# A smaller first token group in a fused attention and feed-forward kernel: batch 0's first 256 queries go first

## The chip, the cores and the metric

The kernel runs on one core of one Trainium2 chip. The metric is device time in microseconds (us), from the first to the last instruction, so lower is better. A few words for the engines: PE is the tensor engine, ACT is ScalarE, DVE is VectorE, POOL is GpSimd, and SP is SyncE, which here only starts transfers.

## The reference

Two stages, with the output of the first as the input of the second.

```python
# q, k, v: (8 batches, 12 heads, 448 tokens, 64), float32
scores = (1 / sqrt(64)) * q @ k.transpose(0, 1, 3, 2)
attn   = maximum(scores, 0) ** 2 / 448
x      = (attn @ v).transpose(0, 2, 1, 3).reshape(3584, 768)
# w_in: (768, 2048), w_out: (2048, 768)
h   = x @ w_in
out = (h * sigmoid(1.702 * h)) @ w_out      # (3584, 768), float32
```

There is no softmax: every score is clipped at zero and squared by itself.

## The kernel before

**Units of work.** Four heads of one batch are a *quad*; there are 3 quads for each batch, 24 in all. A quad's q and k are transposed, then come seven *score slots*, one for each block of 64 keys: PE makes scores, ACT clips them (`rl`, relu), DVE squares them (`at`), and after the seventh slot PE multiplies by v (`av`) and DVE copies the result into `xt`, the input of the feed-forward stage. That stage works on *token groups* of several 64-token blocks. For each group there are 16 chunks of the first product (`ht`, 6 matmuls each; ACT applies the GELU, POOL scales into `gt`), and for each 128 tokens two output chunks (`op`, 16 matmuls each; DVE scales into `osb`, which is stored). PE's order is written out by hand. A *visit* puts up to three attention items between the feed-forward chunks.

The list of groups, in blocks of 64 tokens, and the buffers that the argument needs (3 PSUM buffers for scores and values, 2 for products and transposes):

```python
gblk = [6, 8] * (B // 2)
...
ps_s = ctx.enter_context(tc.tile_pool(name="ps_s", bufs=3, space=bass.MemoryType.PSUM))
ps_m = ctx.enter_context(tc.tile_pool(name="ps_m", bufs=2, space=bass.MemoryType.PSUM))
```

Quads 0 to 5 are loaded by POOL and transposed by PE. From quad 6 on the loads, the transposes and the stores are all started by SP:

```python
def load_qk(u):                       # quads 6 and on
    ...
        nc.sync.dma_start(out=x, in_=quad(t, b, pr))
def trans(u):
    ...
        nc.sync.dma_start_transpose(out=t[:, :, :], in_=...)
def store(g, m, lo, hi, engs): ...    # m2() passes (nc.sync, nc.sync)
def sp_gate(src):                     # SP waits here until src is there
    nc.sync.dma_start(out=gate[0:1, :], in_=src)
```

The opening. All 21 slots of batch 0 come first, then group 0's first product with quads 3 to 5 in between, then the gate with the first loads for SP, and then group 0's first output chunks:

```python
while pos[0] < b0:
    visit(1)                          # quads 0 to 2, transposes of 1, 2, 3 after slots 4, 11, 19
    ...
for f in range(NF):
    m1(0, f)
    if f in (2, 8):
        trans_pe(4 + f // 8, "k", 0)
        trans_pe(4 + f // 8, "q", 0)
    ...
    if f % 2 == 1 or f > 12:
        visit(min(3, b1 - pos[0]))
while pos[0] < b1:
    visit(min(3, b1 - pos[0]))
...
sp_gate(wout[0][1][0:1, 0, 0:64])
prefetch(8, 0)                        # q, k, v of quads 6 and 7 (SP, POOL)
for m in range(gblk[0] // 2):
    m2(0, m, 0)                       # the h = 1 halves are mixed into group 1
```

## Time and profile before

| | before |
|---|---|
| time, median of the first 3 runs | 409.68 us (408.52 to 409.70) |
| PE busy | 383.3 of 406.5 us (94%) |
| last `xt` copy releases group 0's first product | 32.15 us |
| group 0's first product and quads 3 to 5 done | 64.04 us |
| first slot of quad 6 | 77.81 us |
| group 1's first product and group 0's outputs done | 113.95 us |
| from there to the end | 292.6 us, PE nearly always full (busy for 287.7 us) |

How to read it: after 114 us only PE's own work counts. What the change can win lies in the first 114 us, where the trace has PE busy for 95.6 us and idle for 18.3. The lines themselves stand in the prediction below.

### The profile page before, as it was taken

The page shows a single profiled execution, that of the slowest core. Times are in us where ns is not written, and L with a number is a line of the kernel's source. Part 1 is how long each engine was busy: PE and PEld are TensorE (multiplying, and loading weights), DVE is VectorE, ACT ScalarE, POOL GpSimd, SP SyncE. Part 2 cuts the span into 40 slices and gives each one's busy share as a digit, 9 for nine tenths or more (in the row PEclk, how much of TensorE's full clock was granted, in tenths as well). Part 3 has the DMA queues.
Part 4 walks back from the last instruction along what each step waited for, and adds up shares of the span by engine and source line. Part 5 has one row for each costly group of instructions (what it writes and reads, how often), then busy time and mean ns, then how long its engine had stood idle before and what let it go on. Part 6 is the DMA issues. An engine that isn't in the chain of part 4 may idle for free.

```text
span 406.5 us, 7792 instructions
## 1 busy us (share of the span) xinstructions
PE 383.3 (94%) x3192; PEld 202.2 (50%) x3192; DVE 190.7 (47%) x294; ACT 205.3 (51%) x297; POOL 130.8 (32%) x200
## 2 busy tenths in 40 slices
PE   3777899899999999999999999999999999999995
PEld 2433455344455455444455555444455555455564
DVE  0894763267746565564466455546354321010121
ACT  4984771576866454556475446546745511322100
POOL 8453424434433143244133324312311222323100
PEclk9989999999999999999999999999999999999999
DMA  8999997589775653955747396845121111111133
GB/s 122 194 204 205 205 290 153 115 192 246 184 173 111 165 139 72 261 106 134 183 70 166 71 198 153 197 51 82 40 52 35 39 40 40 40 39 40 39 79 78
DMA packets 65220, 50.85 MB, mean 125 GB/s; under 512 B 35744, under 2 KB 61728, under 8 KB 65184
## 3 DMA queue, kind: packets, MB, share of 16 engines
q1 hardware_dynamic: 47792, 35.60, 35.5%
q0 software_dynamic: 17152, 14.55, 24.0%
q8 instruction: 25, 0.41, 0.4%
q10 hardware_dynamic: 240, 0.20, 0.2%
q14 instruction: 11, 0.09, 0.1%
HBM read 45.61 MB, written 11.01 MB: 139 GB/s over the span
## 4 chain that ended last, share of the span: by engine, by line
PE 84%; DVE 6%; ACT 5%; issue 2%; DMA 2%; POOL 0%; ACTq 0%; DVEq 0%; POOLq 0%
PE op L278 35%; PE ht L249 33%; PE sc L144 7%; PE av L169 7%; ACT rl L158 4%; DVE at L159 3%; DMA q<-in_q_dram 1%; DVE rl L155 1%; DVE xt L186 1%; DMA qT<-q 1%; ACT gf L254 1%; DVE kT L134 1%; DVE k L101 0%; POOL gt L256 0%; PE tr L127 0%
## 5 line engine op out<-in xcount | busy, mean ns | idle before, releaser
L158 ACT ACTIVATE rl<-sc 128x896 f16<-128x896 f32 x165 | 144.8, 920 | 49.7 <-PE sc L144 49.7
L249 PE MATMUL ht<-xt,win 128*128 128x384 f16 (+1 forms) x768 | 158.4, 353 | 4.4 <-DVE kT L134 3.4
L159 DVE TENSOR_TENSOR at<-rl 128x896 f16<-128x896 f16 x168 | 114.9, 692 | 87.7 <-ACT rl L158 87.4
L256 POOL TENSOR_SCALAR gt<-gf 128x384 f16<-128x384 f32 (+1 forms) x128 | 77.6, 606 | 235.7 <-ACT gf L254 234.7
L278 PE MATMUL op<-wout,gt 128*128 128x384 f16 (+1 forms) x912 | 153.2, 323 | 0.0
L254 ACT ACTIVATE gf<-ht 128x384 f32<-128x384 f32 (+1 forms) x128 | 70.4, 550 | 119.6 <-PE ht L249 106.8
L278 PEld LDWEIGHTS <-gt 128*128 128x128 f16 x912 | 88.0, 98 | 60.5 <-issue 2.7
L249 PEld LDWEIGHTS <-win 128*128 128x128 f16 x768 | 71.1, 98 | 81.6 <-issue 21.4
L284 DVE TENSOR_SCALAR osb<-op 128x384 f32<-128x384 f32 (+1 forms) x57 | 31.3, 549 | 108.0 <-PE op L278 106.5
L144 PE MATMUL sc<-qT,kT 64*64 64x448 f16 x672 | 48.6, 367 | 6.8 <-DVE qT L134 3.0
L169 PE MATMUL av<-at,v 64*64 64x448 f16 x672 | 38.0, 360 | 2.3 <-ACT rl L158 1.4
L144 PEld LDWEIGHTS <-kT 64*64 64x64 f16 x672 | 17.5, 107 | 33.2 <-issue 22.9
L186 DVE CAST xt<-av 128x768 f16<-128x768 f32 (+2 forms) x36 | 26.9, 774 | 8.4 <-PE av L169 8.3
L169 PEld LDWEIGHTS <-v 64*64 64x64 f16 x672 | 20.1, 109 | 16.9 <-issue 7.1
L88 POOL DMA_DIRECT2D v<-in_v_dram x24 | 17.9, 745 | 5.2 <-DMA win<-in_moe_w_in_dram 2.9
L101 POOL CAST q<-qst 128x896 f16<-128x896 f32 x18 | 16.9, 941 | 0.3
L101 DVE CAST k<-kst 128x896 f16<-128x896 f32 x18 | 14.0, 785 | 0.0
L127 PE MATMUL tr<-ident,k 128*64 128x128 f16 x84 | 4.2, 253 | 5.2 <-DMA k<-in_k_dram 5.2
L134 DVE COPY qT<-tr 128x896 f16<-128x896 f16 (+1 forms) x6 | 3.4, 572 | 7.0 <-ACT qT L132 7.0
L127 PEld LDWEIGHTS <-k 128*64 128x64 f16 x84 | 3.1, 128 | 6.9 <-DMA k<-in_k_dram 5.2
L296 POOL DMA_DIRECT2D win<-in_moe_w_in_dram x8 | 5.4, 674 | 2.3 <-DMA q<-in_q_dram 1.3
L116 POOL DMA_DIRECT2D q<-in_q_dram x6 | 4.3, 713 | 3.0 <-PE sc L144 1.3
(17 smaller groups left out, 26.2 us busy)
## 6 DMA issues: line engine op xcount, KB each, us to landing
out_dram<-osb SPq DMA_DIRECT2D x54, 192.0 KB, 2.7
kst<-in_k_dram SPq DMA_DIRECT2D x18, 448.0 KB, 4.9
qst<-in_q_dram SPq DMA_DIRECT2D x18, 448.0 KB, 5.6
v<-in_v_dram POOLq DMA_DIRECT2D x24, 224.0 KB, 4.7
win<-in_moe_w_in_dram POOLq DMA_DIRECT2D x8, 384.0 KB, 11.5
wout<-in_moe_w_out_dram POOLq DMA_DIRECT2D x4, 768.0 KB, 12.1
k<-in_k_dram POOLq DMA_DIRECT2D x6, 224.0 KB, 8.9
q<-in_q_dram POOLq DMA_DIRECT2D x6, 224.0 KB, 8.9
```

The lines of the kernel that those rows point to most:

```text
L88: nc.gpsimd.dma_start(out=x, in_=quad(v, b, pr))
L101: eng.tensor_copy(out=o, in_=i)
L144: nc.tensor.matmul(out=sc[c, a, 0:S], lhsT=st["kT"][r, j, c], rhs=st["qT"][r, :, c], start=True, stop=True)
L158: nc.scalar.activation(out=rl, in_=sc[:, :, 0:S], func=AF.Relu)
L159: nc.vector.tensor_tensor(out=at, in0=rl, in1=rl, op=ALU.mult)
L169: nc.tensor.matmul(out=st["av"][64 * a:64 * a + 64, s, 0:S], lhsT=st["v16"][r, a, 64 * j:64 * j + 64], rhs=at[r, a, :], start=(j == 0), st ...
L186: nc.vector.tensor_copy(out=xts[g][:, 2 * pr:2 * pr + 2, 64 * (lo - gcum[g]):64 * (hi - gcum[g])], in_=av[:, :, 64 * (lo - b * J):64 * (hi ...
L249: nc.tensor.matmul(out=ht[:, 0:n], lhsT=w[:, kk, fo:fo + 128], rhs=xts[g][:, kk, 0:n], start=(kk == 0), stop=(kk == NK - 1))
L254: nc.scalar.activation(out=gf[:, 0:n], in_=ht[:, 0:n], func=AF.Gelu_apprx_sigmoid, scale=1.0 / SC)
L256: nc.gpsimd.tensor_scalar(out=gts[g][:, f, 0:n], in0=gf[:, 0:n], scalar1=SC, scalar2=1.0, op0=ALU.mult, op1=ALU.mult)
L278: nc.tensor.matmul(out=op[:, 0:w], lhsT=gts[g][:, f, m * 128:(m + 1) * 128], rhs=wout[h][f // WO][:, f % WO, part * w:(part + 1) * w], sta ...
L284: nc.vector.tensor_scalar(out=ot[:, lo:lo + w], in0=op[:, 0:w], scalar1=1.0 / SC, scalar2=None, op0=ALU.mult)
```

## The change

The intent: let PE begin the feed-forward product earlier. Group 0 becomes 4 blocks (256 tokens) and needs only the first 256 of 448 queries of quads 0 to 2. Their other 192 queries ("second halves") move between group 0's chunks. All four output chunks of group 0 stand in the opening, none are left to mix into group 1. The transposes stand between score slots, w_out comes in two transfers, and POOL triggers the early loads in one new order.

```diff
-    gblk = [6, 8] * (B // 2)
+    gblk = [4, 8, 6, 8, 6, 8, 6, 6, 4]
...
-    wout = [[cst.tile([128, WO, NOUT], F16, ...) for i in range(NF // WO)] for h in range(2)]
+    wout = [cst.tile([128, NF, NOUT], F16, name=f"wout{h}") for h in range(2)]
...
+    def ranges(u):
+        if u < NP:
+            pairs = [[0, 1], [2, 3], [4, 5], [6]]
+            return [(0, QA, pairs), (QA, S - QA, pairs)]      # QA = 256
+        return [(0, S, [[j] for j in range(J)])]
...
+    half_visits = {1: S_(0, 1, 2, 3) + S_(1, 1, 0), 3: V_(0, 1) + S_(1, 1, 1, 2),
+                   5: S_(1, 1, 3) + S_(2, 1, 0, 1), 8: V_(1, 1) + S_(2, 1, 2, 3),
+                   10: S_(3, 0, 0, 1) + V_(2, 1)}
...
+        pool_work = {0: lambda: load16(4, "q"), 1: lambda: load_v(4),
+                     2: lambda: w2(0), 4: lambda: load16(5, "k"),
+                     6: lambda: load16(5, "q"), 8: lambda: load_v(5), 10: lambda: w2(1)}
+        trans_at = {6: (3, "k"), 7: (3, "q"), 14: (4, "k"), 15: (4, "q")}
+        more = {12: 3, 14: 2}
         for f in range(NF):
             m1(0, f)
+            if f in half_visits:
+                visit_of(half_visits[f])
...
+        visit(3)
+        m2(0, 0, 0)
+        visit(3)
+        m2(0, 1, 0)
+        trans_pe(5, "k")
+        visit(2)
+        trans_pe(5, "q")
+        visit(3)
+        visit(3)
+        visit(2)
+        m2(0, 0, 1)
+        visit(1)
+        m2(0, 1, 1)
...
-        sp_gate(wout[0][1][0:1, 0, 0:64])
+        sp_gate(units[5]["q16"][0:1, 0, 0, :])
         prefetch(8, 0)
-        for m in range(gblk[0] // 2):
-            m2(0, m, 0)
...
-            moe.append((x, 1000.0 if i < 3 else 2.6))
+        for f in range(NF):
+            moe.append((("m1", 1, f), 1000.0 if f < 2 else 2.3))
```

## The prediction

Where the text is marked as cut, it gave 2 us for halving three quads (part 6; not a term of the sum), and all terms with the price of a 256-column chunk, a shape that the trace before does not have. That price can be estimated from the trace: the chain has 1.95/12 = 162.5 ns a matmul for 384 columns and 3.88/18 = 215.6 for 512, and a straight line through the two gives 109 ns for 256, or 0.656 us a chunk. With this estimate the cut terms read 16 x 0.656 = 10.5 us in part 2, whose PE work came to 18.8, and 16 x (0.98 - 0.656) = 5.2 in the sum. So 10.4 us were subtracted from 113.95, the change stood 3.4 us behind, and the sum came to 412.2, given as 411.5. The 1.03 us for 1024 elements on ACT in part 1 lies on the line through the trace's 0.60 for 512 and 0.92 for 896.

> **What bounds the kernel now.** I read the page's slice table first, then the chain of waits in order of time, then the table by stretches, then the timeline of the stretches where the tensor engine (PE) was not full. In the slice table (one digit per 10.2 us, tenths busy) PE is at 7 to 8 in the first four slices while VectorE (DVE) and ScalarE (ACT) are there at 7 to 9; afterwards PE is at 9.
>
> ```profile
> PE   3777899899999999999999999999999999999995
> DVE  0894763267746565564466455546354321010121
> ACT  4984771576866454556475446546745511322100
> ```
>
> Stretches (us; busy us of each engine, count, then clock and DMA share): from 133.6 to 378.7 PE never stops. So only the opening, one stall near 131 and the tail can be shortened; everything between is pure matmul time.
>
> ```profile
> core 0: us, PE busy (x) PEld busy (x) DVE busy (x) ACT busy (x) POOL busy (x), PEclk, DMA share, GB/s
> 34.00:50.00 16.00, 13.27 (x166) 7.23 (x159) 10.73 (x16) 10.53 (x17) 7.84 (x12) 1.00 1.29 204
> 133.60:325.30 191.70, 191.70 (x1586) 99.11 (x1585) 99.98 (x150) 107.99 (x156) 57.52 (x86) 1.00 0.52 115
> 325.30:378.70 53.40, 53.40 (x318) 28.93 (x318) 6.67 (x11) 12.89 (x23) 13.16 (x23) 1.00 0.15 38
> ```
>
> The chain (start, length) gives clean prices from the full part: 16 op matmuls 2.60; six ht matmuls of 512 columns 3.88/3 = 1.29, of 384 1.95/2 = 0.98; three score slots 0.69 (0.23 a slot), an attention-value unit 1.32 to 1.45.
>
> ```profile
> 331.46 1.95 PE ht L249 x12
> 333.41 2.60 PE op L278 x16
> ...
> 351.59 3.88 PE ht L249 x18
> ```
>
> The opening in the timeline (start, length, engine, operation, idle before and its releaser):
>
> ```profile
> 8.95 3.35 ACT L158 ACTIVATE rl<-sc 128x896 f16<-128x896 f32 x4 [1.08 <-PE sc L144]
> 24.76 5.07 ACT L158 ACTIVATE rl<-sc 128x896 f16<-128x896 f32 x6 [0.30 <-PE sc L144]
> 32.15 1.46 PE L249 MATMUL ht<-xt,win 128*128 128x384 f16 x8 [0.30 <-DVE xt L186]
> 38.39 1.14 PE L249 MATMUL ht<-xt,win 128*128 128x384 f16 x6 [1.84 <-DVE kT L134]
> 50.86 1.14 PE L249 MATMUL ht<-xt,win 128*128 128x384 f16 x6 [1.55 <-DVE kT L134]
> 77.81 0.76 PE L144 MATMUL sc<-qT,kT 64*64 64x448 f16 x12 [0.63 <-DMA qT<-q]
> ```
>
> Until 32.15 the first token group waits for all seven score slots of three head quads: 23 relu evictions on ACT at 0.84 each (3.35/4) run nearly without a gap. Later PE stops twice because a transpose's PSUM buffer is not yet copied out: the copy stands behind three squares in DVE's order. Adding up PE's work until group 1's first product and group 0's last output chunk are done (113.95: the 32 first-product chunks of groups 0 and 1, 6 output chunks, 66 slots, 9 attention-value units, 12 transposes) gives 16 x 0.98 + 16 x 1.29 + 6 x 2.60 + 66 x 0.23 + 9 x 1.4 + 12 x 0.58 = 86.7 us; with some 3 us for changes between operations (about 0.09 each), 24 us are lost there, 5.2 of them the wait for the first k.
>
> [...] 2.60/16 = 162.5 ns for 384 columns, and 14 transposes took 0.58. [...] the trace has 0.92 for 896 elements, 0.60 for 512, and 0.84 back to back. [...] in the trace two squares beside a GpSimd cast of q (130.53 to 131.47) took 2.55 instead of 1.2, which delays everything behind them on DVE and stops PE from 132.9 to 133.56:
>
> ```profile
> 129.95 2.55 DVE L159 TENSOR_TENSOR at<-rl 128x896 f16<-128x896 f16 x2 [2.25 <-ACT rl L158]
> 133.56 1.14 PE L249 MATMUL ht<-xt,win 128*128 128x384 f16 x6 [0.66 <-DVE osb L284]
> ```
>
> That case is one stall, some 1.8 us with its wake. [...] the trace's DMA share is full up to 50 us, at some 200 GB/s, so what matters is the order of the loads.
>
> **The change part by part.**
> 1. The first group shrinks from 6 to 4 blocks of 64 tokens and needs only 256 of 448 queries of each of three quads. Score slots become pairs of key blocks (1024 elements), 4 per quad. ACT needs 9 x 1.03 + 3 x 0.60 + 0.82 = 11.9 us before the first product instead of 23 x 0.84 = 19.3. DVE becomes the limit: 6 transpose copies x 0.62, 9 squares x 0.69 (estimate from 0.63 for 896), 3 x 0.43, 3 evictions x 0.69, and the first two slots of the second half, which stand ahead of the last eviction (relu on DVE included, 2.1): 15.4 us, from 6.2 on. I then walked the engines' orders by hand: an instruction starts when the one before it on its engine is done (ACT 0.09 and DVE 0.05 earlier, as back to back in the trace), its inputs are there, and the buffer it takes (3 for scores and values, 2 for products and transposes) has been read out; 0.05 from one engine to the next, a score pair 0.5 until ACT can start. It runs: quad 0's q copied 7.87; first relu 8.60 to 9.63; quad 1's q copied 11.87, its last square 17.97; quad 2's q copied 15.73, its last relu done 20.94, its squares to 21.55; second-half slots 21.0 to 23.8 on ACT and DVE; last xt eviction 23.75 to 24.4; first product done 24.7, against 32.6 before.
> 2. The rest of those three quads (17 key blocks of 192 queries) moves into group 0's first product[...]. The same walk: chunks 0, 4, 8, 12 end at 24.7, 29.3, 35.6, 40.8, chunk 15 at 45.3, and quad 4's q is copied at 48.4, i.e. 24.0 us: the second transpose of each pair waits for the first one's DVE copy (1.6 us at quad 3, 2.4 plus 0.7 at quad 4), because both PSUM buffers of that pool are taken; the copies stand behind a DVE relu and up to four squares, as at 38.39 before.
> 3. Then 14 slots, 3 attention-value units, 2 transposes and all 4 output chunks of group 0: PE 14 x 0.23 + 3 x 1.4 + 2 x 0.58 + 4 x 2.60 = 19.0. The output chunks no longer fill the waits evenly: about ten slots lie between two pairs of chunks. Hand walk: 24.1 us, with waits of 2.4 (copy of quad 5's q), 1.5 and 1.2 (three score buffers, the value eviction and a DVE relu in front). End 72.5.
> 4. Group 1's first product: 16 x 1.29 + 24 slots x 0.23 + 3 x 1.4 = 30.4, now without output chunks between. Quad 6's k is cast after the last output eviction; from cast to landed q transpose it took 77.68 - 72.51 = 5.2 before, so the first visit waits some 1.9. ACT has 24 x 0.84 + 16 x 0.51 = 28.3, close enough to PE's 30.4 to cost waits at three score buffers. Hand walk: 34.5, end 107.
> 5. Loads: k and q of quad 3 and v move behind two more w_in quarters, w_out becomes two transfers. Landing one after the other at 200 GB/s, I place w_in's third quarter at 31.5 (needed at 35), its last at 35.4 (needed at 40), the first w_out half at 46.7 (needed at 50), the second at 58 (needed at 66). Hidden, with a thin margin.
> 6. Smaller groups add almost no PE time[...]. The tail's last group of 4 instead of 8 changes nothing: PE is full there.
>
> **The sum.** At 107 the new kernel has done two blocks less of the first product[...] and two output chunks less (5.2). The kernel before stood at that amount of work at 113.95 - 10.4 = 103.6. So the change is 3.4 us behind there. The stall near 131 (1.8) may or may not return with other boundaries: I take half. Result: 409.7 + 3.4 - 0.9 = 412.2; I give 411.5, because the hand walk's waits are each a little uncertain and the order was evidently chosen to avoid them.
>
> **Rivals.** (a) The gain stays: the first product begins 8 us earlier and little is given back; then 401 to 404. For it: the opening is the only place with idle PE, and 8 us is what the earlier start shows. Against: PE work is conserved, the 17 key blocks and their evictions come back in stages 2 and 3, and there ACT and DVE must still do them between chunks that are a third shorter. (b) Loads bind: a late w_in quarter, or GpSimd held in its in-order queue by a load trigger while group 0's scaling waits; then stage 2 stretches by 3 to 6 and the time is 415 to 418. For it: DMA share full until 50. Against: the margins of part 5. (c) Group 1 becomes ACT-bound: without output chunks between, 28.3 against 30.4; [...] 2 to 4 more, 414 to 416. (d) Everything cancels, 408 to 413: this is my centre.
>
> **Range and chances.** Errors of the hand walk of 1 to 2 us in each of four stages give about 4 us; that and rival (a) set the low end at 404, (b) and (c) the high end at 418. Faster by over 2% needs under 401.5, that is nearly all of the 8 us kept: 0.08. Slower needs over 417.9: 0.10. Within: 0.82.
>
> **What would show it.** First ht near 24.7 (its wait on the xt eviction): right if within 1.5. Group 0's first product ended near 45 and waits of PE on kT and qT copies of 1.5 to 3 us at quads 3, 4 and 5. Group 1's first chunk at 72.5, its first score slot released by the q transpose, group 1 ended near 107. From there PE full and the same prices. Wrong if group 1 ends before 99 (rival a), if PE's waits in stage 2 are on DMA or GpSimd (b), or if PE shows idle time after 140.

## The result, and the profile after

| | before | after |
|---|---|---|
| median of 4 runs each | 409.10 us (407.67 to 409.70) | 429.89 us (427.58 to 432.11) |
| ratio after / before | | 1.0513, 95% interval 1.0449 to 1.0577 |

Slower by 5.1%, outside the predicted range of 404 to 418. Ratios here and below are the mean time of one kernel's fast runs over that of the other's of the same rounds, so not quite the ratio of the medians. The profiled execution of the changed kernel was the slowest of its four (432.11 us).

First the slice table of the changed kernel; a slice is 10.76 us. PE, then the granted clock, then the share of the DMA engines:

```profile
PE   4777878639989999999999999999999999999996
PEclk9988997959999999999999999999999999999999
DMA  8999960696763939656837872952031111111122
```

Before, PE was at 8 or 9 from slice 5 to the last but one. Now there is a hole at slices 8 and 9 (75 to 97 us: 6 and 3). Ahead of it stands a slice with no transfers at all, the 0 at 64.5 to 75.3 us. In that stretch the kernel before was at 5 to 7. A hole in PE that follows a hole in the transfers suggests a load that was started late.

The stages, changed kernel first, then the kernel before. The columns are named in the first line; the last four are PE clock, DMA share and GB/s after the busy times:

```profile
core 0: us, PE busy (x) PEld busy (x) DVE busy (x) ACT busy (x) POOL busy (x), PEclk, DMA share, GB/s
51.00:77.77 26.77, 22.73 (x233) 12.28 (x233) 16.47 (x27) 10.46 (x12) 1.38 (x2) 0.87 0.45 78
77.77:93.08 15.31, 4.05 (x19) 1.69 (x18) 1.81 (x3) 1.79 (x3) 4.47 (x6) 0.79 0.90 248
93.08:124.60 31.52, 30.00 (x258) 12.54 (x258) 19.61 (x28) 25.39 (x36) 14.49 (x19) 0.94 0.78 181
```

```profile
64.04:77.80 13.76, 13.14 (x73) 6.97 (x72) 2.96 (x6) 2.81 (x5) 6.38 (x9) 1.00 0.57 93
77.80:113.95 36.15, 34.57 (x304) 16.32 (x308) 23.46 (x35) 26.56 (x37) 15.19 (x20) 1.00 0.91 198
```

In 15.3 us from 77.77 on PE works for 4. Before, the stage up to quad 6's first slot had PE busy for 13.14 of 13.76 us.

PE's timeline of the changed kernel (start, length, engine, line, operation; in brackets the idle time before it and what ended it):

```profile
24.21 1.03 PE L272 MATMUL ht<-xt,win 128*128 128x256 f16 x8 [2.09 <-DVE xt L202]
...
35.77 1.44 PE L272 MATMUL ht<-xt,win 128*128 128x256 f16 x6 [2.32 <-DVE kT L129]
...
62.83 0.96 PE L152 MATMUL sc<-qT,kT 64*64 64x448 f16 x8 [2.32 <-DVE qT L129]
...
69.32 4.46 PE L301 MATMUL op<-wout,gt 128*128 128x384 f16 x16
...
77.77 4.05 PE L272 MATMUL ht<-xt,win 128*128 128x512 f16 x18
93.08 1.33 PE L152 MATMUL sc<-qT,kT 64*64 64x448 f16 x12 [11.27 <-DMA qT<-q]
```

The first product is released by the last `xt` copy 8 us earlier than before (24.21 against 32.15). The stops at the transposes are still there. The line that matters is the last: PE stands still for 11.27 us until the transposed q of quad 6 lands; before, that stop was 0.63 us. The output chunk at 69.32 takes 4.46 us instead of 2.77, with the granted clock at 0.62 from 69.3 to 73.8 us. Right after the two stops of 2.32 us the granted clock was 0.50 (35.77 to 37.14 us) and 0.52 (62.83 to 66.30), after the stop of 11.27 us it was 0.50 (93.08 to 95.00) and then 0.69 (to 98.00). From 66.30 to 69.32 us, where PE worked for 1.30 of 3.02 us with stops of 0.89 and 0.83, it was 1.00, and then came the 0.62.

The chain of waits of the changed kernel shows why q came late (start, length, engine or transfer):

```profile
75.22 2.72 PE op L301 x16
77.97 0.57 DVE osb L307
...
79.06 0.60 SPq L289
79.70 0.59 SPq L329
80.34 0.59 SPq L78
80.98 4.47 DMA qst<-in_q_dram
85.51 0.93 POOL q L100
...
87.16 5.79 DMA qT<-q
93.08 1.33 PE sc L152 x12
```

SPq is SP's own queue of transfer starts. L289 is a store of group 0's output, L329 the gate, L78 a load of quad 6. So the load of quad 6 starts after the stores, and the last store waits for the last output chunk's eviction (77.97). Then follow in a row load, cast, and transpose. SP's timeline, changed kernel first, then the kernel before:

```profile
74.40 5.26 SPq L289 DMA_DIRECT2D out_dram<-osb  x4
79.70 0.59 SPq L329 DMA_DIRECT2D gate<-q  x1
80.34 0.59 SPq L78 DMA_DIRECT2D kst<-in_k_dram  x1
...
84.94 2.12 SPq L107 DMA_TRANSPOSE kT<-k  x1
87.16 3.19 SPq L107 DMA_TRANSPOSE qT<-q  x1
```

```profile
49.72 0.61 SPq L307 DMA_DIRECT2D gate<-wout  x1
50.39 0.77 SPq L79 DMA_DIRECT2D kst<-in_k_dram  x1
...
73.23 1.33 SPq L108 DMA_TRANSPOSE kT<-k  x1
74.68 1.22 SPq L108 DMA_TRANSPOSE qT<-q  x1
```

Before, the loads of quad 6 started at 50.39 us, 27 us before they were used, and the first stores came only at 86.54 us. In the changed kernel four stores stand first in the same queue, and the load starts at 80.34.

The stages against the prediction, in us: first chunk of the first product done by 24.6, when ACT begins to read it (24.7 predicted), quad 4's q copied at 50.9 (48.4), group 1's first chunk at 77.8 (72.5), group 1 ended at 124.5 (107). The kernel before had that amount of work done at 103.6, so 20.9 us are lost by then. The rest took 305.8 us instead of the 302.9 that the kernel before would need from its point.

### The profile page after: what moved, and what is told of

It reads as the page before. It is cut to its first block, busy times and chain, and to the rows that moved or that the text cites. A ratio compares the mean times of both kernels' runs of the same rounds, so it can differ in the third digit from the quotient of the medians.

```text
span 430.3 us, 8387 instructions
## 1 busy us (share of the span) xinstructions
PE 391.9 (91%) x3456; PEld 216.8 (50%) x3456; DVE 198.2 (46%) x313; ACT 204.5 (48%) x311; POOL 135.2 (31%) x214
## 3 DMA queue, kind: packets, MB, share of 16 engines
q1 hardware_dynamic: 47792, 35.60, 34.5%
## 4 chain that ended last, share of the span: by engine, by line
PE 81%; DVE 7%; ACT 4%; DMA 3%; issue 2%; POOL 1%; SPq 1%; ACTq 0%; POOLq 0%
PE op L301 33%; PE ht L272 32%; PE sc L152 8%; PE av L183 7%; ACT rl L168 4%; DVE at L169 3%; DMA qT<-q 1%; DMA qst<-in_q_dram 1%; DMA q<-in_q_dram 1%; DVE rl L165 1%; PE tr L125 1%; DVE xt L202 1%; DVE k L100 1%; DVE qT L129 1%; DVE osb L307 0%
## 5 line engine op out<-in xcount | busy, mean ns | idle before, releaser
L168 ACT ACTIVATE rl<-sc 128x896 f16<-128x896 f32 (+3 forms) x165 | 142.9, 909 | 74.0 <-PE sc L152 73.7
L272 PE MATMUL ht<-xt,win 128*128 128x384 f16 (+2 forms) x864 | 164.1, 337 | 6.4 <-DVE xt L202 3.4
L169 DVE TENSOR_TENSOR at<-rl 128x896 f16<-128x896 f16 (+4 forms) x171 | 117.4, 695 | 94.8 <-ACT rl L168 94.3
L279 POOL TENSOR_SCALAR gt<-gf 128x384 f16<-128x384 f32 (+2 forms) x144 | 82.9, 576 | 232.8 <-ACT gf L277 231.0
L277 ACT ACTIVATE gf<-ht 128x384 f32<-128x384 f32 (+2 forms) x144 | 73.1, 507 | 134.7 <-PE ht L272 131.4
L272 PEld LDWEIGHTS <-win 128*128 128x128 f16 x864 | 81.6, 99 | 78.8 <-issue 25.0
L152 PE MATMUL sc<-qT,kT 64*64 64x448 f16 (+2 forms) x756 | 49.8, 349 | 21.2 <-DMA qT<-q 11.3
L183 PE MATMUL av<-at,v 64*64 64x448 f16 (+2 forms) x756 | 38.5, 338 | 0.7 <-DVE at L169 0.6
L202 DVE CAST xt<-av 128x512 f16<-128x512 f32 (+3 forms) x48 | 27.9, 617 | 8.7 <-PE av L183 8.6
L183 PEld LDWEIGHTS <-v 64*64 64x64 f16 x756 | 22.0, 109 | 14.3 <-issue 5.1
L165 DVE TENSOR_SCALAR rl<-sc 128x768 f16<-128x768 f32 (+1 forms) x6 | 6.1, 1017 | 0.0
```

The costliest lines, as they stand in the source:

```text
L152: nc.tensor.matmul(out=sc[c, a, x * n:(x + 1) * n], lhsT=st["kT"][r, j, c], rhs=st["qT"][r, q0 // 64:(q0 + n) // 64, c], start=True, stop= ...
L168: nc.scalar.activation(out=rl[:, :, 0:w], in_=sc[:, :, 0:w], func=AF.Relu)
L169: nc.vector.tensor_tensor(out=at[:, :, 0:w], in0=rl[:, :, 0:w], in1=rl[:, :, 0:w], op=ALU.mult)
L183: nc.tensor.matmul(out=av[64 * a:64 * a + 64, s, 0:n], lhsT=st["v16"][r, a, 64 * j:64 * j + 64], rhs=at[r, a, x * n:(x + 1) * n], start=(j ...
L202: nc.vector.tensor_copy(out=xts[g][:, 2 * pr:2 * pr + 2, 64 * (lo - gcum[g]):64 * (hi - gcum[g])], in_=av[:, :, 64 * (lo - first):64 * (hi ...
L272: nc.tensor.matmul(out=ht[:, 0:n], lhsT=w[:, kk, fo:fo + 128], rhs=xts[g][:, kk, lo:hi], start=(kk == 0), stop=(kk == NK - 1))
```

## The experiments

Theory 1: SP's queue causes most of it; put the loads where they stood and the time returns near the prediction. Theory 2 (rival): the new opening itself, that is the order of DVE's and ACT's work and the low clock after its stops, costs the time. Theory 3 (rival): the new group list alone costs it. Runs below: four of each kernel. "Own before" is the median of the kernel before on the same chip: 409.10 for the changed kernel, 408.76 for the first four experiments, 407.71 for the next four, 407.70 for the third four and 408.57 for the last three.

| kernel | median us | minus own before | ratio to before, 95% interval |
|---|---|---|---|
| changed kernel | 429.89 | +20.8 | 1.0513 (1.0449 to 1.0577) |
| a_loads_first | 427.98 | +19.2 | 1.0447 (1.0379 to 1.0516) |
| a_loads_mix | 422.33 | +13.6 | 1.0342 (1.0310 to 1.0373) |
| b_late_loads | 419.25 | +10.5 | 1.0262 (1.0233 to 1.0290) |
| b_wout2 | 408.33 | −0.4 | 1.0003 (0.9963 to 1.0043) |
| b_groups | 414.35 | +6.6 | 1.0161 (1.0132 to 1.0191) |
| mix_warm | 421.96 | +14.3 | 1.0325 (1.0286 to 1.0364) |
| mix_act | 421.59 | +13.9 | 1.0324 (1.0301 to 1.0348) |
| b_trans_apart | 407.56 | −0.2 | 0.9972 (0.9941 to 1.0003) |
| mix_ops_late | 424.22 | +16.5 | 1.0383 (1.0354 to 1.0413) |
| mix_pace | 419.75 | +12.1 | 1.0268 (1.0231 to 1.0305) |
| a_stores_act | 420.70 | +13.0 | 1.0306 (1.0278 to 1.0335) |
| b_trans_act | 405.17 | −2.5 | 0.9924 (0.9896 to 0.9953) |
| a_nosq (wrong result) | 414.70 | +6.1 | 1.0145 (1.0118 to 1.0171) |
| bg_nosq (wrong result) | 414.78 | +6.2 | 1.0158 (1.0125 to 1.0191) |
| b_nosq (wrong result) | 404.97 | −3.6 | 0.9907 (0.9884 to 0.9930) |

### SP's queue

**a_loads_first**: the changed kernel, with the gate and the loads of quads 6 and 7 moved ahead of the outputs of group 0.

```diff
+        sp_gate(units[5]["q16"][0:1, 0, 0, :])
+        prefetch(8, 0)
         visit(3)
         m2(0, 0, 0)
 ...
         m2(0, 1, 1)
-        sp_gate(units[5]["q16"][0:1, 0, 0, :])
-        prefetch(8, 0)
```

> The changed kernel, with the gate and the loads of quads 6 and 7 placed in SyncE's queue ahead of group 0's four output stores; nothing else moves. Theory 1 (load queue: the loads stood behind stores that wait for output chunks until 77.97): PE's stop of 11.3 us before quad 6's first score slot falls to under 2.5, its cold clock behind it too, and the time falls from 429.9 to 415 to 419. Theory 2 (the opening's own waits and the cold clock cost the time, the loads would have been late anyway): over 425.

Measured: 427.98 us, a miss; the expected gain did not come (three executions at 427 to 429, one at 422.64). SP's timeline of this run says why:

```profile
49.04 0.76 SPq L78 DMA_DIRECT2D kst<-in_k_dram  x1
...
74.69 5.26 SPq L289 DMA_DIRECT2D out_dram<-osb  x4
79.99 0.59 SPq L78 DMA_DIRECT2D kst<-in_k_dram  x1
80.62 0.51 SPq L78 DMA_DIRECT2D qst<-in_q_dram  x1
81.26 1.34 SPq L107 DMA_TRANSPOSE kT<-k  x1
82.70 2.67 SPq L107 DMA_TRANSPOSE qT<-q  x1
```

The loads do start at 49 us, but quad 6's transposes, and two loads of quad 8 ahead of them, are in the same queue and still stand behind the four stores. PE's stop shrank from 11.27 to 7.32 us. So the edit had treated only half of the cause.

**a_loads_mix**: as well, the second halves of group 0's output chunks go back between group 1's chunks, as before, which moves the stores out of the way.

```diff
...
-        m2(0, 0, 1)
         visit(1)
-        m2(0, 1, 1)
...
-        for f in range(NF):
-            moe.append((("m1", 1, f), 1000.0 if f < 2 else 2.3))
+        for i, x in enumerate(mix([("m1", 1, f) for f in range(NF)],
+                                  [("m2", 0, m, 1) for m in range(gblk[0] // 2)])):
+            moe.append((x, 1000.0 if i < 2 else 2.3))
```

> As the run with the loads first, and in addition group 0's two second-half output chunks are spread into group 1's first product, as the kernel before does. If group 1 is bound by ACT (my rival c), this gives 2 to 4 us more: 412 to 416. If only the store order mattered, it lies within 1.5 us of the run with the loads first.

Measured: 422.33 us, which neither forecast allowed (412 to 416, or within 1.5 us of a_loads_first); the stop before quad 6 is 2.32 us. Two edits in one, so the next one isolates the stores.

**a_stores_act**: a_loads_first, with group 0's four stores started by ACT instead of SP. Against a_loads_first nothing else moves; against the changed kernel there are two edits, both to the order of transfer starts.

```diff
-            store(g, m, 0, DM, (nc.sync, nc.sync))
+            store(g, m, 0, DM, (nc.scalar, nc.scalar) if g == 0 else (nc.sync, nc.sync))
```

> The run with the loads first (428.0, where quad 6's q transpose still waits behind the four output stores and quad 8's loads on SyncE), with group 0's stores issued from ACT's queue. Theory load queue, second form (what stands behind the stores on SyncE sets group 1's start, first the loads, then the transposes): PE's stop before quad 6 falls from 7.3 to 2 to 3 us and the time to 420 to 423.5. If mixing the chunks and not the queue brought the run with mixing to 422.3: over 426.

Measured: 420.70 us, 7.3 us under a_loads_first (6.2 against own befores), and the stop before quad 6 is 2.81 us. This is PE's line there:

```profile
84.75 0.76 PE L152 MATMUL sc<-qT,kT 64*64 64x448 f16 x12 [2.81 <-DMA qT<-q]
```

Against their own befores the changed kernel is at +20.8 and this one at +13.0. SP's order is therefore worth 7.8 us in this kernel, which fits the stop's 11.27 − 2.81 = 8.5 us.

**b_late_loads**: the same fault put into the kernel before. Its gate waits for the third output tile of group 0 instead of w_out.

```diff
-    gate = cst.tile([1, 64], F16, name="gate")
+    gate = cst.tile([1, 64], F32, name="gate")
...
-        sp_gate(wout[0][1][0:1, 0, 0:64])
-        prefetch(8, 0)
         for m in range(gblk[0] // 2):
             m2(0, m, 0)
+        sp_gate(osb[0, 2][0:1, 0:64])
+        prefetch(8, 0)
```

> The kernel before, with one thing added: the gate on SyncE waits for group 0's last first-half output eviction (near 72.6) instead of w_out (49.7), so the loads of quads 6 and 7 start 23 us later. Theory 1: the first score slot of quad 6 comes some 12.7 us after the loads start, as in the changed kernel (80.3 to 93.1), so at about 85.5 instead of 77.8; the time grows by 6 to 9 us, to 415 to 418. Theory 2: under 2 us.

Measured: 419.25 us, +10.5, somewhat more than expected. PE stops before quad 6 until the same transfer:

```profile
87.50 1.33 PE L144 MATMUL sc<-qT,kT 64*64 64x448 f16 x12 [9.41 <-DMA qT<-q]
```

Late loads alone, with the old opening and the old groups, reproduce the hole. Theory 1 holds, but for 7.8 of 20.8 us in the changed kernel; theories 2 and 3 are needed for the other 13 us.

### Parts that turned out neutral

**b_wout2**: the kernel before with w_out in two transfers.

```diff
...
-        pool_work = {1: lambda: w2(0, 0), 2: lambda: w2(0, 1),
-                     4: lambda: w2(1, 0), 5: lambda: w2(1, 1)}
+        pool_work = {1: lambda: w2(0), 4: lambda: w2(1)}
...
-        sp_gate(wout[0][1][0:1, 0, 0:64])
+        sp_gate(wout[0][0:1, 8, 0:64])
```

> The kernel before with w_out in two transfers of 1536 KB instead of four of 768 KB, issued after chunks 1 and 4. Both theories: no difference beyond 1 us (409 to 410), since w_out lands before it is used. If larger transfers cost or win by themselves, it would show here.

Measured: ratio 1.0003. The number of transfers of w_out does not matter here.

**b_trans_apart**: the kernel before with the k transposes of quads 4 and 5 one chunk ahead of the q transposes.

```diff
+            if f in (1, 7):
+                trans_pe(4 + f // 7, "k", 0)
             if f in (2, 8):
-                trans_pe(4 + f // 8, "k", 0)
                 trans_pe(4 + f // 8, "q", 0)
```

> The kernel before with one part of the change's idea alone: the k transposes of quads 4 and 5 one first-product chunk ahead of their q transposes instead of both together. If the part is worth something in itself, PE's stops at 38.39 and 50.86 (1.84 and 1.55 us) shrink below 0.8 each and the time falls 1 to 2 us, to 407 to 408. If it only moves the stop to another chunk: 408.3 to 410.

Measured: ratio 0.9972, interval up to 1.0003: a gain of at most some tenths of a per cent. The two stops at kT are gone, but PE now stops 0.74 and 0.86 us at the copies of q.

### The group list

**b_groups**: the kernel before with the new list of groups and nothing else.

```diff
-    gblk = [6, 8] * (B // 2)
+    gblk = [4, 8, 6, 8, 6, 8, 6, 6, 4]
```

> The kernel before with only the list of token groups of the change (4, 8, 6, 8, 6, 8, 6, 6, 4 blocks instead of 6, 8 four times); its opening still does the whole first batch first. In the last run a first-product chunk of 256 columns took 2.16/3 = 0.72 us in the full part[...]. If the list costs only that: 410 to 412. If a smaller first group also leaves the attention of quads 3 to 5 without product work to hide in[...]: 413 to 416. If the list is neutral, as I predicted: 408 to 410.

On the straight line's 0.656 us, 32 chunks at 0.72 are some 2 us dearer, which is what "only that" means, and the first group's 16 chunks would be 5.2 us lighter than before (measured 4.2).

Measured: 414.35 us, +6.6. The prediction had said that smaller groups add almost no PE time. The stretch from the first product until quads 3 to 5 and group 0's chunks are done lasted 31.2 us (31.17 to 62.41), against 31.9 (32.15 to 64.04) in the kernel before, although its 16 chunks had shrunk by about 4.2 us (0.98 to 0.72 each). So that product work had been nearly free where it stood. The new list moves it to a part where PE is full, and there it costs its full time: after the stretch b_groups needs 350.2 us and the kernel before 342.5. Of these 7.7 us more, the moved chunk work is 4.2, and the whole list's product chunks are 2.4 dearer at the clean prices (147.7 us against 145.3).

Where the 4.2 us went inside the stretch, the two stage lines show (kernel before first, then b_groups):

```profile
32.15:64.04 31.89, 27.49 (x309) 14.36 (x308) 20.18 (x30) 19.77 (x31) 11.82 (x19) 1.00 1.21 239
31.17:62.41 31.24, 25.80 (x308) 15.36 (x308) 19.93 (x32) 18.83 (x31) 10.25 (x19) 0.89 1.24 242
```

PE's busy time fell by only 1.7 us, with the granted clock at 0.89 instead of 1.00, and PE's idle time grew from 4.4 to 5.4 us. All four executions of b_groups show a lower clock over the whole run (0.984 to 0.992) than those of the kernel before (0.994 to 1.000).

The 256-column chunk is also dearer than the straight line through 384 and 512 columns. Two lines of the full part of a_loads_mix give its clean price, from start to start:

```profile
378.06 2.28 PE L272 MATMUL ht<-xt,win 128*128 128x256 f16 x18
380.22 2.76 PE L301 MATMUL op<-wout,gt 128*128 128x384 f16 x16
```

That is 2.16 us for 18 matmuls, 120 ns each or 0.72 us a chunk; the line gives 109 ns and 0.656. For the 32 chunks of two 4-block groups that makes some 2 us.

**b_nosq, bg_nosq, a_nosq**: the next question is what those stretches wait for. In these three kernels quads 3 to 5 are not squared: ACT writes the relu straight to where the square would stand. Their outputs are wrong, which doesn't matter for the times. It takes 21 squares and three relus from DVE; the three relus go to ACT.

```diff
     def relu2(...):
+        if NP <= u < 2 * NP:
+            at = atp.tile(...)
+            nc.scalar.activation(out=at, in_=sc, func=AF.Relu)
+            return at
```

From the kernel before:

> Wrong result on purpose. The kernel before (407.7), without the squares of quads 3 to 5. Group 0's product is larger here, so PE has less slack to win: 2 to 4 us (404 to 406). If its gain equals that with the new list, the list's 6.6 us have nothing to do with DVE.

Measured: 404.97 us, 3.6 under its before, as expected.

From b_groups:

> Wrong result on purpose. The kernel before with the new group list (414.35), without the squares of quads 3 to 5. Theory DVE chain is what the new opening adds: this gains less than the changed kernel does, 3 to 5 us (409.5 to 411.5). Rival: the same gain in both.

Measured: 414.78 us, no gain, a miss. The total would say that DVE does not bound the stretch, but the trace says otherwise. These are PE's lines of bg_nosq:

```profile
54.81 5.36 PE L282 MATMUL op<-wout,gt 128*128 128x384 f16 x32
60.01 5.34 PE L253 MATMUL ht<-xt,win 128*128 128x512 f16 x24
72.44 1.34 PE L144 MATMUL sc<-qT,kT 64*64 64x448 f16 x12 [7.08 <-DMA qT<-q]
```

The stretch ended at 54.81 instead of 62.41 us, 7.6 us earlier. Then PE stood 7.08 us at quad 6, because its loads had not become earlier: in both kernels SP's gate opens when w_out has landed (49.46 and 49.67 us). In b_groups this stop was 0.65 us. So a bound of 7 us was removed and the next one, the loads, took its place.

The lengths of the stretch settle the question that the totals could not:

| stretch from first product to end of group 0's chunks | with squares | without |
|---|---|---|
| old list (before, b_nosq) | 31.9 | 28.5 |
| new list (b_groups, bg_nosq) | 31.2 | 24.4 |
| saved by the smaller chunks | 0.7 | 4.1 |

Without DVE's squares the 4.2 us of smaller chunks show almost in full; with them 0.7 shows. In bg_nosq PE's stops at the copies are gone, the granted clock is 1.00 again and PE is busy for 22.4 us instead of 25.8. So DVE's squares, with the three relus, are what hides the shorter product. They do it mostly by way of the clock: from the old list to the new, PE's busy time falls by 4.8 us without them (27.3 to 22.4) and by 1.7 with them, and the idle time grows by 1.0 with them. Whether the stretch would have stayed as long at full clock, with PE waiting for DVE instead, no run separates.

From a_stores_act:

> Wrong result on purpose. The changed kernel with group 0's stores on ACT's queue (420.7), and without the squares of quads 3 to 5 (21 DVE instructions of 0.6 us, and DVE's three relus there, which ACT does): PE's stops behind transpose copies vanish. Theory DVE chain: 6 to 9 us faster, 412 to 415. Rival (fixed order, waits for buffers and for ACT): under 3 us, 418 to 421.

Measured: 414.70 us, 6.0 less (6.9 against own befores), within the range expected. Group 1's first chunk starts 8.9 us earlier (68.92 against 77.82), although PE now waits 0.97 us for w_out before it. Part of that goes again: the two chunks after quad 6's first slots take 4.45 us instead of 2.76, and at the end of the two traces 7.3 us are left. As it now equals bg_nosq in time, one could say that only the squares separate the openings. That would be wrong, since bg_nosq loses 7 us at another bound.

### The new opening

The difference that is left is between a_stores_act (+13.0) and b_groups (+6.6), 6.4 us on the same list with SP's queue out of the way. Four experiments tried single suspects. All four start from a_loads_mix (+13.6), so they bear on the 6.4 us only as far as the two variants are alike.

**mix_warm**: 50 small matmuls without use ahead of the first slots of quads 4, 5 and 6. It tests whether the low clock after the stops there costs the time: in the changed kernel the granted clock was 0.52 after the 2.32 us stop at quad 5's q (62.83 to 66.30 us), and quad 4's value unit, which follows, took 2.81 us instead of 1.52.

```diff
+    WARM = {(4, 0, 0): 10, (5, 0, 0): 20, (6, 0, 0): 20}
...
+        for _ in range(WARM.get((u, p, i), 0)):
+            nc.tensor.matmul(out=sc[:, 0, 0:128], lhsT=ident[:, :], rhs=ident[:, :],
+                             start=True, stop=True)
```

> The run with loads first and output chunks mixed, plus dummy matmuls (10, 20 and 20 of 128 columns) into the score buffer that PE is about to fill, ahead of the first slots of quads 4, 5 and 6, where PE waits for a transpose copy. Theory clock (waits let the clock drop, and the work after them runs slow): quad 4's value unit, 2.89 us there, falls to about 1.5, and the time by 1 to 3 us, to 419.5 to 421.5. Theory no clock effect: 422 to 424.

Measured: ratio 1.0325 against 1.0342, intervals overlapping: inconclusive. The trace says more than the total. Quad 4's value unit took 1.52 us instead of 2.89, as the clock theory said, and the way from quad 5's first slot to group 1's first chunk took 8.11 us instead of 9.05. But this execution had lost 1.5 us before that, with a granted clock of 0.72 around quad 3's transposes (35 to 41 us), where the traced execution of a_loads_mix had 1.00. So the clock costs time here, and it differs between executions; the total cannot show how much.

**mix_act**: the relus and the transpose copies of quads 3 to 5 go from DVE to ACT.

```diff
-        nc.vector.tensor_copy(out=t, in_=ps[:, 0:J * 128])
+        if u >= NP:
+            nc.scalar.activation(out=t, in_=ps[:, 0:J * 128], func=AF.Copy)
+        else:
+            nc.vector.tensor_copy(out=t, in_=ps[:, 0:J * 128])
```

> The run with loads first and output chunks mixed, with the relus of quads 3 to 5 that DVE does and the transpose copies of quads 3 to 5 moved to ACT, which was busy 9.3 of 21 us between 51 and 72 where DVE was busy 16.2. Theory DVE chain (PE's stops in the opening are transpose copies standing behind squares and relus on DVE): 3 to 5 us faster, 417 to 419.5. Theory of a mere order problem, which ACT has as well: within 1 us of 422.3.

Measured: 421.59 us, ratio 1.0324; hardly a gain, a miss. PE still stopped 1.61, 1.0 and 2.42 us at copies, now those on ACT: there a copy stands behind relus as it stood behind squares on DVE.

**mix_ops_late**: the two output chunks that stand among quad 5's slots go behind them.

```diff
         visit(3)
-        m2(0, 0, 0)
         visit(3)
-        m2(0, 1, 0)
 ...
         visit(1)
+        m2(0, 0, 0)
+        m2(0, 1, 0)
```

> The run with loads first and output chunks mixed, with group 0's two first-half output chunks moved from between quads 4 and 5 to after quad 5's values. If the opening is set by the attention's chain through ACT and DVE, output chunks between its slots are free, and moving them out costs most of their 5.2 us: 425 to 427.5. If they delay that chain (my part 3: about ten slots are left between two pairs of chunks), it is faster: 419 to 421.

Measured: 424.22 us. Against own befores +16.5 instead of +13.6. Quad 5's values end at 67.03 instead of 70.24 us, so two chunks of together 5.2 us had cost 3.2 where they stood. They were partly hidden; these two lumped chunks are not the fault.

**mix_pace**: visits in group 1 every 2.6 us of product work, as in the kernel before, not every 2.3.

```diff
-            moe.append((x, 1000.0 if i < 2 else 2.3))
+            moe.append((x, 1000.0 if i < 2 else 2.6))
```

> The run with loads first and output chunks mixed, with the visits in group 1 paced 2.6 us apart, as the kernel before has them, instead of 2.3. If the tighter pace is what makes PE wait at three score buffers between 111.7 and 115.1, 1 to 2 us faster (420.5 to 421.5); if group 1 is bound by ACT whatever the pace, within 0.7 of 422.3.

Measured: 419.75 us, 2.6 less than a_loads_mix, or 1.5 less against own befores. The tighter pace costs something in this variant; in a_stores_act it was not tried.

No single edit removes the 6.4 us. The traces give an account of it, which no experiment has tested term by term. With four output chunks at 2.70 us subtracted, a_stores_act has its other opening work done at 77.82 − 10.8 = 67.0 us, b_groups at 62.41, so 4.6 later. PE's work other than output chunks was busy 0.9 longer (45.47 against 44.53), one of the four output chunks, at a low clock (0.61), took 1.7 longer (4.45 against 2.77), and PE was idle 1.9 longer. After that the stop before quad 6 is 2.2 us longer (2.81 against 0.65).

### A version faster than both

**b_trans_act**: b_trans_apart, with the copies of quads 4 and 5 on ACT.

```diff
+            if f in (1, 7):
+                trans_pe(4 + f // 7, "k", J)
             if f in (2, 8):
-                trans_pe(4 + f // 8, "k", 0)
-                trans_pe(4 + f // 8, "q", 0)
+                trans_pe(4 + f // 8, "q", J)
```

> A candidate to beat both: the kernel before with the transposes of quads 4 and 5 apart by one chunk and their PSUM copies on ACT instead of DVE. The copies no longer stand behind squares and a relu on DVE: PE's stops of 1.84 and 1.55 us fall under 0.5 each; 406 to 407.5, against 407.6 with the transposes apart alone. If ACT's own queue holds them as long: 407.5 to 409.

Measured: 405.17 us with a correct result, ratio 0.9924 (0.9896 to 0.9953). The two stops at kT of 1.84 and 1.55 us are gone; 0.17 us is left. In the old opening ACT's order has room for these copies at those places. It is 0.8% faster than the kernel before and, by the two ratios, 5.6% faster than the changed one.

## Why the prediction was wrong

The prediction said 411.5 us; it is 429.9. By its own steps:

1. **First product at 24.7**: right. The last `xt` copy releases it at 24.21, and ACT begins to read the first chunk at 24.63.
2. **Stage 2 until quad 4's q is copied, 48.4**: 2.5 us too early (50.9). The stops were where it said and about as long in all (2.32 us at quad 3 instead of 1.6, 1.66 at quad 4 instead of 3.1). It had priced all matmuls at full clock; the granted clock from 24.2 to 51 us was 0.87, and PE was busy for 22.2 us instead of 18.8.
3. **Stage 3 until group 1's first chunk, 72.5**: this stage alone is 2.7 us longer than predicted. Again the clock was 0.87, and PE was busy for 22.7 us instead of 19.0; one output chunk took 4.46 instead of 2.77 us and one value unit 2.8 instead of 1.5.
4. **Group 1 in 34.5 us with a first wait of 1.9**: this is the step that failed most: the stage took 46.7 us, 12.2 more, of which 9.4 are that first wait. It measured from quad 6's cast to its landed transpose, and took for granted that the loads had long arrived, as before. It had read DVE's order but not SP's: the stores of four output chunks stand there ahead of the loads, and the wait was 11.27 us. a_stores_act shows that 7.8 us of the total are due to that order, and b_late_loads that late loads alone do this in the old kernel.
5. **Loads hidden**: right for the weights; the changed kernel's profile has no PE wait on w_in or w_out, and b_wout2 was neutral. It left out the loads of quad 6.
6. **Smaller groups cost almost nothing; the tail changes nothing**: wrong. b_groups costs 6.6 us. The step priced PE's work as if each microsecond of it weighed the same everywhere, and put the kernel before at equal work at 103.6 by subtracting full chunk prices. But 4.2 us of chunk work in the first stretch was worth only 0.7, with the granted clock there at 0.89 and longer stops. The price of the 256-column chunk (0.656 us on the straight line, measured 0.72) is a smaller part of the same error. From the end of group 1 on the changed kernel needed 2.9 us more than expected; about 1.0 of that is the 256-column chunks of the last group, the rest was not separated.

**The sum as it turned out**, against own befores: 7.8 us from SP's order, 6.6 from the list of groups, 6.4 from the new opening on that list; together 20.8. They add up by construction: the first two are measured, SP's order by two edits of transfer starts in the changed kernel, the list by a single edit in the old opening, and the third is what is left over. That the list costs the same in both openings was not tested. Of the third, the experiments show that the squares bound the stretch (8.9 us shorter without them) and rule out the two output chunks lumped among quad 5's slots; how much belongs to the low clock, the split into halves and the first wait for quad 6 is only an account from traces.

Of the rivals, (b) had the right kind of cause, loads held behind another transfer start, but named POOL's queue and the weights instead of SP's and quad 6. Rival (a) was right that 8 us are won at the first product; nothing of it was kept. Rival (c), group 1 bound by ACT, does not show: after quad 6's first slot PE is busy for 30.0 of 31.5 us and ACT for 25.4. The stall near 131 us, counted half: the same wait of 0.66 us for an output eviction comes at 150.44, and PE waits another 1.29 us for an `xt` copy at 126.77. What made that copy late was not looked into.

Two readings in the prediction are loose. PE's first four slices read 3, 7, 7, 7 and not "7 to 8", and ACT's 4, 9, 8, 4; and the 24 us "lost" are 18.3 us of idle time and the rest slow work.

## What to carry to other kernels

When a piece of work moves earlier, walk the queue of every engine that it touches, also of the one that only starts transfers: a store that waits for its data holds every load and transpose written behind it (here SP's four stores began at 74.40 us and quad 6's first load at 80.34; before, that load began at 50.39). Work beside a bound of another engine can be cheap (here 4.2 us of it were worth 0.7), so making it smaller or moving it to where the tensor engine is full can cost time even if the total of its work stays about the same (the new list alone cost 6.6 us). When an experiment removes a suspected bound and the total does not move, measure the stretch itself before clearing the suspect, for the next bound may have taken the gain.
